# The first sixth of a fused attention and two-layer FFN kernel, issued from one list of 430 named operations

## The chip, the cores and the metric

The kernel runs on one core of one Trainium2 chip. The metric is the device time of one launch in microseconds (us), the median of several runs.

The engines are named as in the profile. PE is TensorE, which does the matmuls. PEld is its weight load, DVE is VectorE, ACT is ScalarE, POOL is GpSimd. SP issues most of the transfers. SPq and ACTq are the queues on which SP and ACT issue DMAs. Each engine works through its own instructions in program order, and semaphores make it wait for other engines or for transfers.

## The reference

`moe` and `moe2` are plain two-matrix layers over all tokens. There are 3072 tokens (4 batches of 768), model width 384 and inner width 2048. All numbers are float32.

```python
def _attn_ref(q, k, v, alpha):            # (4, 8, 768, 48) each
    state = np.zeros((B, H, D, D))
    for t in range(S):
        state = alpha[:, :, t, :, None] * state + np.einsum('bhd,bhe->bhde', k[:, :, t], v[:, :, t])
        y[:, :, t] = np.einsum('bhd,bhde->bhe', q[:, :, t], state)
    return y

def _moe_ref(x, w_in, w_out):
    h = x @ w_in
    g = np.maximum(0.01 * h, h)
    return g @ w_out

def _moe2_ref(x, w_in, w_out):
    h = x @ w_in
    g = np.where(h > 0.0, h, np.exp(np.minimum(h, 0.0)) - 1.0)
    return g @ w_out
```

The output is `_moe2_ref(_moe_ref(attention rows))`.

## The kernel before, in words

**Units and blocks.** A unit is 128 consecutive tokens of one batch, with all eight heads. There are 24 units, and four of them make a block of 512 tokens. The recurrence over a unit is done with matmuls. DVE builds running products of alpha with two scans, `E` and `F` (`prep_k`, `prep_F`), and scales k and q with them (`prep_k`, `prep_q`). PE forms the scores (`attn_sc`), DVE masks them (`attn_mask`), and PE forms the output (`attn_po`). The state goes from unit to unit: PE transposes k (`attn_pk`), ACT copies it out (`attn_kn`), PE multiplies it with v (`attn_pu`), and DVE adds it to the scaled old state (`attn_T` or `attn_carry`, then `attn_state`).

**Rows of x.** A unit's output is written as a high part (`attn_xh`, ACT) and the rest (`attn_rest` on PE and `attn_xl_act` on ACT in the first two blocks, `attn_xl` on DVE later). When the last unit of a block is done, `gather` moves some of the rows to other partitions with DMAs (`x<-x` in the profile). The block's FFN products read x only after that.

**FFN of layer 1.** The inner width is cut into 16 tiles m. `ffn1_h(j, m)` is a group of nine 128x512 matmuls for block j: for each of three 128-row parts of x, the products wh·xh, wl·xh and wh·xl (w is split into a high part wh and a low part wl, as x is). ACT copies the sum out (`ffn1_t`), DVE takes the maximum (`ffn1_max`), ACT rounds it to gh (`ffn1_gh`), DVE forms the rest gl (`ffn1_gl`). `ffn1_y(j, m)` is a second group of nine matmuls, from gh and gl into three sums `y` that collect over m.

**Conversion of the weights.** The weights come as 64-bit words. `stage1(m)` loads the words of tile m with five DMAs. Two ACT passes (`convert_p`), three DVE passes and an ACT cast to wh (`convert_a`), and a DVE subtraction for wl (`convert_b`) turn them into the two parts. In layer 1 all 16 tiles are converted in the first 151 us.

**Order.** Up to about 150 us the order is written out by hand: `quarter(u, i)` issues a quarter of unit u's attention and part of the preparation of unit u + 1, and `conv1.p`, `conv1.a`, `conv1.b` issue the conversions up to a number. Blocks 0 and 1 share this stretch. From `s = 4` to `s = 16` the main loop takes over with one y group, one h group and a conversion each. From `s = 17` on it issues an h group, an attention piece (`attn_pe` on PE, `attn_post` on ACT and DVE) and a y group per step. `in_order` then pins every engine to the order in which the code issued its instructions. Blocks 2 to 5 have their attention in the main loop, and layer 2 follows.

**Pools.** `pack` (alpha, k and q of a unit) and `v` have three buffers each. Two PSUM banks serve the h groups, three the y sums, three all of attention. Most of attention's intermediate tiles have one buffer.

Of the kernel before, what the change touches and what calls it, by code (L numbers as in the profile page):

```python
# [19 lines left out]
def attention_two_layers_kernel(  # L20
# [124 lines left out]
    def prep_k(u):  # L145
# [6 lines left out]
        pe = pe_p.tile([PR, NP, 1], F32, tag="pe", name="pe")  # L152
        nc.vector.tensor_scalar(pe, ext(E, 0)[:, :, 1:2], 1e24, 1e-24, ALU.min, ALU.max)
        nc.vector.reciprocal(ext(d1, 0)[:, :, 0:1], pe)
        e2 = E[:, 1:EXT].rearrange("p (g c) -> p g c", c=C + 1)
        nc.vector.tensor_mul(kS, kS, e2[:, :, 1:C + 1])
        st[u] = dict(kS=kS, qh=qh, pe=pe, alpha=al)
# [41 lines left out]

    def attn_mask(u):  # L200
        d = st[u]
        A = at_p.tile([128, 2, NP, C], F32, tag="A", name="A")
        for j, sc in enumerate(d.pop("sc")):
            nc.vector.tensor_mul(A[:, j], sc, causal.unsqueeze(1).to_broadcast([128, NP, C]))
        d["A"] = A

# [122 lines left out]
    def convert_p(raw, tp, ts, hi, lo):  # L329
        words = raw.rearrange("p (f t) -> p f t", t=2)  # L330
        rest = raw.bitcast(U16).rearrange("p (f t) -> p f t", t=4)[:, :, 1]
        nc.scalar.activation(tp.bitcast(F32), words[:, :, 1].bitcast(F32), ACTF.Copy, scale=2.0 ** -112)
        nc.scalar.activation(words[:, :, 0], rest, ACTF.Copy, scale=2.0 ** -13)

    def convert_a(raw, tp, ts, hi, lo):
        words = raw.rearrange("p (f t) -> p f t", t=2)
        nc.vector.tensor_scalar(ts, words[:, :, 1], -0x80000000, None, ALU.bitwise_and)
        nc.vector.scalar_tensor_tensor(  # L338
            out=tp, in0=tp, scalar=3, in1=ts, op0=ALU.logical_shift_left, op1=ALU.bitwise_or)
        nc.vector.tensor_tensor(out=ts, in0=tp, in1=words[:, :, 0], op=ALU.add)  # L340
        nc.scalar.copy(hi, ts.bitcast(F32))  # L341

    def convert_b(raw, tp, ts, hi, lo):
        nc.vector.tensor_sub(lo, ts.bitcast(F32), hi.bitcast(F32))

# [11 lines left out]
    def ffn1_h(j, m, ahead=0):  # L357
        xh, xl, n, _ = xt[j]
        hp = hbank(n, "hp")
        fill(hp, ahead)  # L360
        wh, wl = win[m]
        i = 0
        for kk in range(KD):
            for a, x in ((wh, xh), (wl, xh), (wh, xl)):
                nc.tensor.matmul(hp, lhsT=a[:, kk, :], rhs=x[:, kk, :n], start=(i == 0), stop=(i == 3 * KD - 1))  # L365
                i += 1
        steps[1, j, m] = hp

    def ffn1_t(j, m):
        t = g_p.tile([128, xt[j][2]], F32, tag="t", name="t")  # L370
        nc.scalar.copy(t, steps[1, j, m])  # L371
        steps[1, j, m] = t

    def ffn1_max(j, m):
        t = steps[1, j, m]
        nc.vector.scalar_tensor_tensor(out=t, in0=t, scalar=0.01, in1=t, op0=ALU.mult, op1=ALU.max)  # L376

    def ffn1_gh(j, m):
        gh = gs_p.tile([128, xt[j][2]], F32R, tag="gh", name="gh")
        nc.scalar.copy(gh, steps[1, j, m])  # L380
        steps[1, j, m] = steps[1, j, m], gh

    def ffn1_gl(j, m):
        t, gh = steps[1, j, m]
        gl = gs_p.tile([128, xt[j][2]], F32R, tag="gl", name="gl")
        nc.vector.tensor_sub(gl, t, gh.bitcast(F32))  # L386
        steps[1, j, m] = gh, gl
# [6 lines left out]

    FIRST = 4
# [5 lines left out]
    def ffn1_y(j, m):  # L401
        n = xt[j][2]
        gh, gl = steps.pop((1, j, m))
        first, last = parts(j, m)
        if first:
            ytiles[j] = [ps_y.tile([128, n], F32, tag=f"y{c}", name=f"y{c}") for c in range(KD)]
        wh, wl = wout[m]
        for c in range(KD):
            for i, (a, x) in enumerate(((wh, gh), (wl, gh), (wh, gl))):
                nc.tensor.matmul(  # L410
                    ytiles[j][c], lhsT=a[:, c * 128:(c + 1) * 128], rhs=x,
                    start=(first and i == 0), stop=(last and i == 2),
                )
        if last:
            t0 = blocks[j][0] * C
            dst = x2t[t0 // 512][:, :, t0 % 512:t0 % 512 + n]
            for c in range(KD):
                if j < 2 and m == KF - 1:
                    nc.vector.tensor_add(dst[:, c], ytiles[j][c], dst[:, c])
                elif c == 1 and j > 1:  # L420
                    nc.vector.tensor_copy(dst[:, c], ytiles[j][c])
                else:
                    nc.scalar.copy(dst[:, c], ytiles[j][c])  # L423
# [125 lines left out]
    def attn_post(u, i):  # L549
# [10 lines left out]
        else:  # L560
# [13 lines left out]
    def next_load(u):  # L574
        if u < NU:
            load_unit(u, eng=nc.scalar)
            load_v(u, eng=nc.scalar)
# [34 lines left out]
    def conv_args(layer, kind, m):  # L612
        i = kind == "out"
        w = (wout if i else win)[m]
        n = nconv[0] % (4 if layer == 1 else 3)
        nconv[0] += 1
        if layer == 1:
            tt = x2t[4 + n % 2].rearrange("p c f -> p (c f)").bitcast(I32)
            return staged[1, m], tt[:, 0:768], tt[:, 768:1536], both[m][0], both[m][1]
# [8 lines left out]

    class Conversions:
        def __init__(self, order):  # L630
            self.order = order
            self.done = [0, 0, 0]
            self.open = {}

        def p(self, upto):
            for i in range(self.done[0], min(upto, len(self.order))):
                self.open[i] = conv_args(1, *self.order[i])
                convert_p(*self.open[i])
                self.done[0] += 1

        def a(self, upto):
            self.p(upto)
            for i in range(self.done[1], min(upto, len(self.order))):
                convert_a(*self.open[i])
                self.done[1] += 1
                m = self.order[i][1]
                if m >= 2 and m + 2 < KF:
                    stage1(m + 2)

        def b(self, upto):  # L650
            for i in range(self.done[2], min(upto, self.done[1])):
                convert_b(*self.open.pop(i))
                kind, m = self.order[i]
                self.done[2] += 1


    class Flow:
# [8 lines left out]
        def start(self, k):  # L666
            raw, tp, ts, hi, lo = self.args[k] = conv_args(2, *self.order[k])
            words = raw.rearrange("p (f t) -> p f t", t=2)
            rest = raw.bitcast(U16).rearrange("p (f t) -> p f t", t=4)[:, :, 1]
            return [  # L670
                lambda: nc.scalar.activation(tp.bitcast(F32), words[:, :, 1].bitcast(F32), ACTF.Copy, scale=2.0 ** -112),
                lambda: nc.scalar.activation(words[:, :, 0], rest, ACTF.Copy, scale=2.0 ** -13)]
# [14 lines left out]
        def go(self, n):  # L687
            for i in range(n):
# [462 lines left out]
```

## Time and profile before

| | us |
|---|---|
| median of 3 runs | 937.37 (936.42 to 939.64) |
| profiled execution, its own time | 935.22 |
| its span, first to last instruction | 933.4 |
| PE busy | 898.0 (96%) |
| DVE busy | 542.7 (58%) |
| ACT busy | 449.9 (48%) |
| mean granted TensorE clock | 0.992 |

Busy shares are means over the whole span. The page of the profile also gives them in 40 slices of 23.3 us each. The first seven of them, about 160 us, hold the attention of the first eight units, the conversion of layer 1's weights, and the first FFN groups of blocks 0 and 1.

### The profile page before, as it was taken

The numbers are of one execution on the slowest core, as the hardware profiler recorded it, in microseconds if no ns is written. First come the engines' busy times: TensorE is split into PE (matmuls) and PEld (weight loads), VectorE is DVE, ScalarE is ACT, GpSimd is POOL, SyncE is SP. The second block draws the span as 40 slices with busy tenths as digits, with TensorE's granted clock in tenths as the row PEclk, the third lists the DMA queues.
The fourth block names the chain that finished last, engine by engine and source line by source line (L and its number), as shares of the span: only waits on it lengthen the run. The fifth ranks groups of instructions, "written<-read, shape, count | busy, mean of one in ns | idle before, by whom it ended". The sixth has DMA issues, their size and how long they took to land.

```text
span 933.4 us, 13414 instructions
## 1 busy us (share of the span) xinstructions
PE 898.0 (96%) x5283; PEld 732.0 (78%) x5283; DVE 542.7 (58%) x909; ACT 449.9 (48%) x816; POOL 1.4 (0%) x11
## 2 busy tenths in 40 slices
PE   7788999999999999999999999999999999999996
PEld 5666767787887878788888888888888888888896
DVE  7897787674665566376368888533433443443332
ACT  2545764222322322322357788746556566566442
POOL 0000000000000000000000000000000000000000
PEclk9999999999999999999999999999999999999999
DMA  9865431313123031321323242121110200200201
GB/s 239 211 181 148 128 111 28 84 44 77 43 77 86 1 86 43 77 78 35 98 72 104 84 119 62 31 46 31 30 34 21 54 11 21 54 21 1 34 1 38
DMA packets 55047, 63.97 MB, mean 69 GB/s; under 512 B 35456, under 2 KB 35968, under 8 KB 54976
## 3 DMA queue, kind: packets, MB, share of 16 engines
q1 hardware_dynamic: 51024, 49.61, 20.9%
q10 hardware_dynamic: 3952, 13.43, 5.3%
q8 instruction: 43, 0.70, 0.3%
q14 instruction: 28, 0.23, 0.1%
HBM read 54.37 MB, written 4.72 MB: 63 GB/s over the span
## 4 chain that ended last, share of the span: by engine, by line
PE 83%; DVE 8%; ACT 3%; DMA 3%; SPq 1%; issue 1%; ACTq 0%; DVEq 0%
PE hp L441 21%; PE y L410 18%; PE hp L365 16%; PE o L490 11%; PE oa L490 7%; PE oa L505 3%; PE po L256 2%; PE sc L228 2%; DVE x2t L338 1%; DMA x2t<-in_w_dram 1%; DVE x2t L340 1%; DMA x<-x 1%; PE o L505 1%; DVE E L151 1%; PE pu L275 1%
## 5 line engine op out<-in xcount | busy, mean ns | idle before, releaser
L365 PE MATMUL hp<-x,w 128*128 128x512 f32 x864 | 215.3, 393 | 7.5 <-DMA x<-x 4.7
L441 PE MATMUL hp<-x,w 128*128 128x512 f32 x864 | 212.3, 390 | 0.0
L365 PEld LDWEIGHTS hp<-x,w 128*128 128x128 f32 x864 | 162.2, 189 | 45.4 <-ACT w L341 4.8
L441 PEld LDWEIGHTS hp<-x,w 128*128 128x128 f32 x864 | 161.8, 188 | 33.4 <-DVE w L698 0.2
L410 PE MATMUL y<-gh,w 128*128 128x512 f32 x576 | 184.4, 401 | 3.6 <-ACT gh L380 2.9
L454 DVE SCALAR_TENSOR_TENSOR t<-t,hp 128x512 f32<-128x512 f32 x96 | 65.9, 687 | 144.0 <-ACT t L449 143.6
L380 ACT CAST gh<-t 128x512 fp32r<-128x512 f32 x96 | 59.7, 622 | 169.1 <-PE y L410 114.1
L386 DVE TENSOR_TENSOR gl<-t,gh 128x512 fp32r<-128x512 f32 x96 | 66.3, 691 | 111.8 <-ACT gh L380 111.2
L410 PEld LDWEIGHTS y<-gh,w 128*128 128x128 f32 x576 | 105.0, 189 | 29.3 <-ACT gh L380 4.9
L410 PE MATMUL y<-gl,w 128*128 128x512 f32 x288 | 113.3, 393 | 1.0 <-DVE gl L386 1.0
L465 DVE TENSOR_TENSOR gl<-t,gh 128x512 fp32r<-128x512 f32 x96 | 66.5, 692 | 66.0 <-ACT gh L459 66.0
L371 ACT COPY t<-hp 128x512 f32<-128x512 f32 x96 | 56.2, 586 | 100.0 <-PE hp L365 99.9
L448 ACT ACTIVATE t<-hp 128x512 f32<-128x512 f32 x96 | 57.3, 597 | 81.3 <-PE hp L441 81.3
L459 ACT CAST gh<-t 128x512 fp32r<-128x512 f32 x96 | 59.7, 622 | 69.7 <-PE o L490 22.8
L490 PE MATMUL o<-gh,w 128*128 128x512 f32 x288 | 88.8, 389 | 0.1
L376 DVE SCALAR_TENSOR_TENSOR t<-t 128x512 f32<-128x512 f32 x96 | 66.0, 687 | 37.8 <-ACT t L371 35.7
L410 PEld LDWEIGHTS y<-gl,w 128*128 128x128 f32 x288 | 54.3, 189 | 14.2 <-DVE gl L386 2.6
L490 PEld LDWEIGHTS o<-gh,w 128*128 128x128 f32 x288 | 54.0, 188 | 11.7 <-ACT x2t L423 0.5
L449 ACT ACTIVATE t<-t 128x512 f32<-128x512 f32 x96 | 60.7, 632 | 3.1
L490 PE MATMUL oa<-gh,w 128*128 128x512 f32 x192 | 59.1, 389 | 0.0
L490 PE MATMUL o<-gl,w 128*128 128x512 f32 x144 | 56.0, 389 | 0.0
L490 PEld LDWEIGHTS oa<-gh,w 128*128 128x128 f32 x192 | 36.0, 188 | 7.5
(130 smaller groups left out, 866.3 us busy)
## 6 DMA issues: line engine op xcount, KB each, us to landing
stg<-in_w_dram SPq DMA_DIRECT2D x28, 384.0 KB, 3.1
pack<-in_seqs_dram ACTq DMA_DIRECT2D x13, 674.2 KB, 5.0
x2t<-in_w_dram SPq DMA_DIRECT2D x20, 384.0 KB, 3.6
span<-in_seqs_dram SPq DMA_DIRECT2D x24, 226.2 KB, 2.6
pack<-in_seqs_dram SPq DMA_DIRECT2D x8, 674.2 KB, 7.3
x2t<-in_w_dram SPq DMA_DIRECT2D x32, 144.0 KB, 2.7
out_dram<-osb SPq DMA_DIRECT2D x60, 64.0 KB, 2.0
vt<-in_vals_dram ACTq DMA_DIRECT2D x13, 288.0 KB, 5.3
```

The costliest lines, as they stand in the source:

```text
L365: nc.tensor.matmul(hp, lhsT=a[:, kk, :], rhs=x[:, kk, :n], start=(i == 0), stop=(i == 3 * KD - 1))
L376: nc.vector.scalar_tensor_tensor(out=t, in0=t, scalar=0.01, in1=t, op0=ALU.mult, op1=ALU.max)
L380: nc.scalar.copy(gh, steps[1, j, m])
L386: nc.vector.tensor_sub(gl, t, gh.bitcast(F32))
L410: nc.tensor.matmul(ytiles[j][c], lhsT=a[:, c * 128:(c + 1) * 128], rhs=x, start=(first and i == 0), stop=(last and i == 2),)
L441: nc.tensor.matmul(hp, lhsT=a[:, kk, :], rhs=x[:, kk, :], start=(i == 0), stop=(i == 3 * KD - 1))
L448: nc.scalar.activation(t, hp, ACTF.Relu, scale=-1.0)
L449: nc.scalar.activation(t, t, ACTF.Exp, scale=-1.0)
L454: nc.vector.scalar_tensor_tensor(out=t, in0=t, scalar=-1.0, in1=hp, op0=ALU.add, op1=ALU.max)
L459: nc.scalar.copy(gh, t)
L465: nc.vector.tensor_sub(gl, t, gh.bitcast(F32))
L490: nc.tensor.matmul(otiles[j][c], lhsT=a[:, c * 128:(c + 1) * 128], rhs=x, start=(m == 0 and i == 0), stop=(m == KF - 1 and i == 2),)
```

## The change

The hand-written order up to `s = 16` is replaced by one string, `STARTUP`, of 430 names. Each name is a single operation on one engine (or a set of DMAs) with its unit, tile or block: `E.5` is the first scan of unit 5, `hA.0.3` the first part of h group (0, 3), `hi.7` the cast of tile 7's weights. A table `first` maps the names to functions, a loop calls them, and `in_order` pins the result. For this, `prep_k` is cut into `prep_E`, `prep_pe` and `prep_kS`, `attn_mask` into two halves, and the conversion into seven functions of one pass each.

An FFN group can now be issued in two parts. For h these are the six matmuls with wh and then the three with wl. For y they are the six with gh and then the three with gl. In the list all h and y groups are issued so. The matmuls themselves and their number stay.

In the main loop, the attention pieces are advanced by one at `s = 17` and `s = 18`, and a second piece of one step is issued behind the y group. In blocks 2 to 5, the last unit of a block now forms its low part and issues the gather ahead of the state update. Its loads for a later unit go behind the gather on SP's queue and not on ACT's queue.

```diff
+    def ffn1_h(j, m, ahead=0, halves=(0, 1)):
         xh, xl, n, _ = xt[j]
-        hp = hbank(n, "hp")
-        fill(hp, ahead)
+        if 0 in halves:
+            steps[1, j, m] = hp = hbank(n, "hp")
+            fill(hp, ahead)
+        hp = steps[1, j, m]
         wh, wl = win[m]
...
+        terms = [(kk, a, x) for kk in range(KD) for a, x in ((wh, xh), (wl, xh), (wh, xl))]
+        if len(halves) == 1:
+            terms = [t for t in terms if (t[1] is wl) == halves[0]]
+        for i, (kk, a, x) in enumerate(terms):
+            nc.tensor.matmul(hp, lhsT=a[:, kk, :], rhs=x[:, kk, :n], start=(0 in halves and i == 0),
+                             stop=(1 in halves and i == len(terms) - 1))
...
+    STARTUP = """
+        E.0 pe.0 F.0 kS.0 q.0 E.1 sc.0 pk.0 pe.1 kn.0 F.1 kS.1 mask0.0 q.1 pk.1 pu.0 mask1.0 E.2 sc.1 kn.1 more.0
...
+        S.3 q.4 xh.3 rest.3 E.5 xl.2 xl.3 j1.1 pk.4 gather.0 p1.2 more.2 kn.4 sc.4 lo.0 hA.0.0.7 hB.0.0 T.4 and.2
...
+        gl.0.10 gh.0.11 j2.14 yB.0.10 and.15 j1.15 hi.14 p2.15 lo.14 j2.15 hi.15 q.8 hA.0.14 hB.0.14 lo.15 piece.8.0
+        gh.0.12 t.0.13 t.0.14 gl.0.11 yA.0.11 gl.0.12 max.0.13 max.0.14 gh.0.13 gh.0.14 post.8.0 gl.0.13 gl.0.14
+        yB.0.11 yA.0.12 yB.0.12
+"""
...
             attn_xh(u, xh, off)
+            ends = u == blocks[j][0] + blocks[j][1] - 1
+            if ends:
+                attn_xl(u, xh, xl, off)
+                gather(t, blocks[j][1] * C, swapped=True)
             attn_state(u)
             if not last:
                 attn_carry(u + 1)
-            attn_xl(u, xh, xl, off)
+            if not ends:
+                attn_xl(u, xh, xl, off)
             st.pop(u)
-            if u == blocks[j][0] + blocks[j][1] - 1:
-                gather(t, blocks[j][1] * C, swapped=True)
-            next_load(u + 3)
+            next_load(u + 3, nc.sync if ends else nc.scalar)
...
+        for name in STARTUP.split():
+            f, *args = name.split(".")
+            first[f](*map(int, args))
         in_order()
...
-        pieces = [(u, i) for u in range(UB + blocks[1][1], NU) for i in range(3)]
+        pieces = [(u, i) for u in range(UB + blocks[1][1], NU) for i in range(3)][1:]
...
-                i, of = (s - KF + 1, KF - LA - 2) if s < 2 * KF else (m + 1, KF - LA - 2)
+                i, of = (s - KF + 1 + (s in (KF + 1, KF + 2)), KF - LA - 2) if s < 2 * KF else (m + 1, KF - LA - 2)
```

**Place 1, PE, from the first FFN group on.** Before: `hp` are the h groups, `w_0_104` and `w_0_105` the high and the low part of tile 0's weights, `w_1_...` those of tile 1, `po` is unit 4's attention output, and the x7 row is filler ahead of the first group.

```order
L354 MATMUL hp<-minus 112x448 x7
L365 MATMUL hp<-x,w_0_104 128x512
L365 MATMUL hp<-x,w_0_105 128x512
L365 MATMUL hp<-x,w_0_104 128x512 x2
L365 MATMUL hp<-x,w_0_105 128x512
L365 MATMUL hp<-x,w_0_104 128x512 x2
L365 MATMUL hp<-x,w_0_105 128x512
L365 MATMUL hp<-x,w_0_104 128x512
L365 MATMUL hp<-x,w_1_106 128x512
```

The same place of the change:

```order
L380 MATMUL hp<-minus 112x448 x7
L394 MATMUL hp<-x,w_0_104 128x512 x6
L394 MATMUL hp<-x,w_0_105 128x512 x3
L265 MATMUL po<-A,vt 64x128
```

The three matmuls with the low part now come last in the group, and unit 4's output stands between the h groups of tiles 0 and 1, where before the two groups followed each other.

**Place 2, SP, around block 0's gather.** Before: `x<-x` is the gather (three of its six DMAs), `x2t_138` and `x2t_139` are the words of weight tiles 2 and 3, `pack` and `vt` are a unit's data. The first `pack` row is unit 6.

```order
L125 DMA pack<-in_seqs_dram 112x1541
L139 DMA vt<-in_vals_dram 128x576
L590 DMA x2t_138<-in_w_dram 48x768
L591 DMA x2t_138<-in_w_dram 16x768
L590 DMA x2t_138<-in_w_dram 48x768
L591 DMA x2t_138<-in_w_dram 16x768
L592 DMA x2t_138<-in_w_dram 128x768
L324 DMA x<-x 16x2x512 x3
L139 DMA vt<-in_vals_dram 128x576
L590 DMA x2t_139<-in_w_dram 48x768
```

And of the change, where unit 6 is the `pack` row behind the gather:

```order
L660 DMA x2t_138<-in_w_dram 128x768
L658 DMA x2t_139<-in_w_dram 48x768
L659 DMA x2t_139<-in_w_dram 16x768
L658 DMA x2t_139<-in_w_dram 48x768
L659 DMA x2t_139<-in_w_dram 16x768
L660 DMA x2t_139<-in_w_dram 128x768
L333 DMA x<-x 16x2x512 x3
L125 DMA pack<-in_seqs_dram 112x1541
L139 DMA vt<-in_vals_dram 128x576
```

Weight tile 3 moved ahead of the gather, and unit 6's load moved from ahead of tile 2 to behind the gather.

**Place 3, DVE, at the end of the conversions.** Before: `w_15_135` is the low part of the last tile, `t<-t` a maximum, `gl` the rest of g, `A` the mask of unit 8, `E` the first scan of unit 9.

```order
L340 ISA x2t_141<-x2t_139,x2t_141 128x1536
L376 SCALAR_TENSOR_TENSOR t<-t 128x512
L344 TENSOR_TENSOR w_15_135<-x2t_141,w_15_134 128x768
L386 TENSOR_TENSOR gl<-t,gh 128x512
L204 TENSOR_TENSOR A<-sc_1394,causal 128x512
L204 TENSOR_TENSOR A<-sc_1395,causal 128x512
L151 SCALAR_TENSOR_TENSOR E<-pack,d_97 112x517
```

And of the change:

```order
L360 ISA x2t_141<-x2t_139,x2t_141 128x1536
L179 TENSOR_TENSOR pack<-pack,F 112x512
L366 TENSOR_TENSOR w_15_135<-x2t_141,w_15_134 128x768
L412 TENSOR_TENSOR gl<-t,gh 128x512 x2
L404 SCALAR_TENSOR_TENSOR t<-t 128x512 x2
L210 TENSOR_TENSOR A<-sc_1356,causal 128x512
L210 TENSOR_TENSOR A<-sc_1357,causal 128x512
L151 SCALAR_TENSOR_TENSOR E<-pack,d_97 112x517
L157 TENSOR_SCALAR pe<-E 112x4
L158 RECIPROCAL d_98<-pe 112x4
L163 TENSOR_TENSOR pack<-pack,E 112x512
L412 TENSOR_TENSOR gl<-t,gh 128x512 x2
```

Two FFN tiles are now in flight behind the last conversion. The two `gl` rows at the end, of tiles 13 and 14, stand behind the mask and the scan, where before only one tile's `gl` followed the conversion and it came ahead of them.

## Rows read from the trace of the kernel before

**Rows 1.** The page's first two parts: busy times, then tenths in 40 slices.
```profile
PE 898.0 (96%) x5283; PEld 732.0 (78%) x5283; DVE 542.7 (58%) x909; ACT 449.9 (48%) x816; POOL 1.4 (0%) x11
...
PE   7788999999999999999999999999999999999996
...
DVE  7897787674665566376368888533433443443332
```
**Rows 2.** Busy time by stretch (us from the start, length, engines, clock, DMA).
```profile
0.00:4.73 4.73, 1.81 (x5) 1.54 (x6) 1.06 (x6) 1.58 (x2) 1.19 (x9) 1.00 0.57 163
4.73:39.84 35.11, 26.89 (x314) 20.87 (x313) 31.64 (x52) 12.06 (x20) 0.00 (x0) 0.95 1.01 250
39.84:78.92 39.08, 33.61 (x281) 25.30 (x281) 34.82 (x57) 18.69 (x30) 0.00 (x0) 1.00 0.53 149
78.92:149.61 70.69, 63.83 (x301) 48.56 (x301) 57.21 (x77) 44.34 (x67) 0.00 (x0) 0.98 0.45 127
149.61:154.48 4.87, 4.38 (x14) 3.17 (x14) 4.80 (x8) 0.71 (x2) 0.00 (x0) 0.65 0.00 0
154.48:200.00 45.52, 43.86 (x395) 35.20 (x393) 29.21 (x53) 13.12 (x29) 0.11 (x1) 1.00 0.22 61
200.00:527.23 327.23, 325.31 (x2186) 263.54 (x2187) 200.76 (x362) 118.81 (x241) 0.11 (x1) 1.00 0.26 68
```
**Rows 3.** PE's waits, 0 to 150 us (total us, times, longest).
```profile
PE pu L275 <- DVE A L204: 4.4, 4, 1.8
PE y L410 <- ACT gh L380: 2.9, 1, 2.9
...
PE hp L365 <- DMA x<-x: 2.8, 2, 2.2
```
**Rows 4.** DVE groups of 0 to 154.48 us: mean ns, idle before and its releaser.
```profile
L344 DVE TENSOR_TENSOR w<-x2t,w 128x768 fp32r<-128x768 f32 x16 | 15.2, 956 | 4.1 <-ACT w L341 4.0
L386 DVE TENSOR_TENSOR gl<-t,gh 128x512 fp32r<-128x512 f32 x19 | 13.0, 686 | 3.8 <-ACT gh L380 3.2 <-PE y L410 0.7
L376 DVE SCALAR_TENSOR_TENSOR t<-t 128x512 f32<-128x512 f32 x19 | 13.0, 686 | 6.7 <-ACT t L371 6.7
L204 DVE TENSOR_TENSOR A<-sc,causal 128x512 f32<-128x512 f32 x18 | 11.5, 682 | 2.1 <-PE sc L182 2.1
L151 DVE TENSOR_TENSOR_SCAN E<-pack,d 112x517 f32<-112x517 f32 x9 | 11.1, 1228 | 2.6 <-DMA pack<-in_seqs_dram 2.6
```
**Rows 5.** Timeline of PE and SP around the first gather and the first h group.
```profile
35.40 2.33 SPq L324 DMA_DIRECT2D x<-x  x3
...
39.84 4.37 PE L365 MATMUL hp<-x,w 128*128 128x512 f32 x18 [2.15 <-DMA x<-x]
```
**Rows 6.** The chain that ended last, one h group behind a y group.
```profile
202.27 2.04 PE hp L365 x9
```
**Rows 7.** DMA issues of 0 to 160 us: median us to landing.
```profile
pack<-in_seqs_dram SPq DMA_DIRECT2D x8, 674.2 KB, 7.3
```
**Rows 8.** Busy time by stretch around PE's two low-clock stretches.
```profile
86.50:89.20 2.70, 2.69 (x6) 2.11 (x7) 2.02 (x4) 1.49 (x3) 0.00 (x0) 0.50 0.86 227
...
147.00:150.60 3.60, 2.34 (x52) 1.48 (x50) 3.17 (x5) 1.94 (x3) 0.00 (x0) 1.00 0.00 0
150.60:154.00 3.40, 3.40 (x9) 2.51 (x9) 3.33 (x7) 0.00 (x0) 0.00 (x0) 0.53 0.00 0
```
**Rows 9.** PE's waits, 149 to 200 us.
```profile
PE pk L190 <- DVE A L204: 1.7, 1, 1.7
PE hp L365 <- ACT w L341: 0.8, 1, 0.8
```
**Rows 10.** PE's waits from 200 us on.
```profile
PE hp L365 <- DMA x<-x: 1.9, 3, 0.9
```
**Rows 11.** Timeline of DVE ahead of a gather of the main loop.
```profile
293.50 0.35 DVE L311 TENSOR_TENSOR S<-pu,carried 112x192 f32<-112x192 f32 x1
293.89 0.36 DVE L218 TENSOR_TENSOR carried<-S,pe 112x192 f32<-112x192 f32 x1
```

More of the change, by code (lines that the diff above doesn't have):

```diff
@@ L198, in attn_kn, with mask_half @@
             d["kn"] = kn
-    def attn_mask(u):
[L201 to L205, printed above, removed]
+    def mask_half(u, j):
+        d = st[u]
+        if "A" not in d:
+            d["A"] = at_p.tile([128, 2, NP, C], F32, tag="A", name="A")
+        nc.vector.tensor_mul(d["A"][:, j], d["sc"][j], causal.unsqueeze(1).to_broadcast([128, NP, C]))
+    def attn_mask(u):
+        mask_half(u, 0)
+        mask_half(u, 1)
     def attn_T(u):
@@ L399, in parts, with ffn1_y @@
         return m == 0 or (j < 2 and m == FIRST), m == KF - 1 or (j < 2 and m == FIRST - 1)
-    def ffn1_y(j, m):
+    def ffn1_y(j, m, copy=True, halves=(0, 1)):
         n = xt[j][2]
-        gh, gl = steps.pop((1, j, m))
+        gh, gl = steps["gh", j, m], steps.get(("gl", j, m))
         first, last = parts(j, m)
-        if first:
+        if first and 0 in halves:
             ytiles[j] = [ps_y.tile([128, n], F32, tag=f"y{c}", name=f"y{c}") for c in range(KD)]
         wh, wl = wout[m]
[L408 to L416, printed above, removed]
-            for c in range(KD):
[L418 to L423, printed above, removed]
@@ new lines, in ffn1_y @@
+        terms = [(c, a, x) for c in range(KD) for a, x in ((wh, gh), (wl, gh), (wh, gl))]
+        if len(halves) == 1:
+            terms = [t for t in terms if (t[2] is not gh) == halves[0]]
+            terms.sort(key=lambda t: t[1] is wl)
+        begun = set()
+        for i, (c, a, x) in enumerate(terms):
+            nc.tensor.matmul(
+                ytiles[j][c], lhsT=a[:, c * 128:(c + 1) * 128], rhs=x,
+                start=(first and 0 in halves and c not in begun),
+                stop=(last and 1 in halves and c not in [t[0] for t in terms[i + 1:]]),
+            )
+            begun.add(c)
@@ new lines, in ffn1_y, with y_copy @@
+        if 1 in halves:
+            del steps["gh", j, m], steps["gl", j, m]
+        if last and copy:
+            for c in range(KD):
+                y_copy(j, m, c)
+    def y_copy(j, m, c):
+        n = xt[j][2]
+        t0 = blocks[j][0] * C
+        dst = x2t[t0 // 512][:, c, t0 % 512:t0 % 512 + n]
+        if j < 2 and m == KF - 1:
+            nc.vector.tensor_add(dst, ytiles[j][c], dst)
+        elif c == 1 and j > 1:
+            nc.vector.tensor_copy(dst, ytiles[j][c])
+        else:
+            nc.scalar.copy(dst, ytiles[j][c])
@@ L627, in conv_args @@
         return raw, tp, ts, flat(w[0]), flat(w[1])
[L629 to L654, printed above, removed]
     class Flow:
@@ L1046, in attention_two_layers_kernel @@
                 post_h(n)
[L1047 removed]
+                for p in now[:1]:
                     attn_pe(*p)
                 if m < KF - 1:
[L1050 removed]
+                    for p in now[:1]:
                         attn_post(*p)
@@ L1053, in attention_two_layers_kernel @@
                 if m == KF - 1:
-                    for p in now:
+                    for p in now[:1]:
                         attn_post(*p)
+                for p in now[1:]:
+                    attn_pe(*p)
+                    attn_post(*p)
             if ph == 2 and m >= KF - 10 and m % 2 == 0:
```

296 lines of the change are left out of this document (98 added, 198 removed).

## The prediction

> **What bounds the kernel now.** I began with the page. PE is busy for 96% of the span, and its slices stand at 9 from the seventh on, except for the last [rows 1]. So only the beginning has time to give. There, PE's slices stand at 7 and 8 and those of DVE mostly between 6 and 8, so neither engine is full, and both are needed.
>
> The busy time by stretch says how much is lost and on whom [rows 2]. I cut at 39.84 us, where the first h group of the FFN starts [rows 5], at 78.92, where block 1's first h group starts, at 149.61, where the h group (0, 15) starts, which is the first group behind the list, and at 154.48, where DVE has done all that the list contains. PE is idle for 39.08 − 33.61 = 5.47 us in the third stretch and 70.69 − 63.83 = 6.86 us in the fourth. DVE, from its first scan at 4.73 to 154.48, is busy for 31.64 + 34.82 + 57.21 + 4.80 = 128.47 us of 149.75 and idle for 21.28.
>
> The waits name the reason. PE waits for masks (4.4 us), for gh (2.9) and for the gathers (2.8) [rows 3], which are things that DVE and ACT make. DVE waits in its turn, for a maximum's input 6.7 us, for ACT's cast of the weights 4.0, for gh 3.2, for scores 2.1 [rows 4], while it has other work further down its own queue: conversions of later tiles, scans of later units. The engines run in order, so that work stays behind the waiting instruction. The loss is one of order, and from 200 us on there is little of it: 327.23 − 325.31 = 1.92 us up to 527.23 [rows 2].
>
> **The change, part by part.** It adds and removes no computation up to the list's end. DVE, ACT and PE run the same passes, and the two parts of an FFN group together are the same nine matmuls. What can change is idle time, so each term is an idle time of before and the part of it that I expect back. All terms are against the profiled execution, 935.22 us. It lies 2.15 below the median of 937.37, so the forecast is that median less the sum.
>
> *Up to the first h group: 0.* The gather of block 0 needs four units of attention in a chain, and was issued at 35.40 [rows 5]. In this stretch DVE is idle for only 35.11 − 31.64 = 3.47 us [rows 2], and the list puts more of units 4 and 5 and of tile 1 ahead of the gather than the old order did. The bounds are 3.47 earlier and, for one more load ahead of the gather on SP (place 2), some 3 later. I take 0, as gains and added work cancel.
>
> *Between the first h group and (0, 15): 10.0.* Two floors limit how early (0, 15) can start. For PE, all its busy time of the third and fourth stretch stays: 33.61 + 63.83 = 97.44, so 39.84 + 97.44 = 137.28 us, which is 12.33 earlier than 149.61. For DVE, the list ends no sooner than 4.73 + 128.47 = 133.20. Behind the last operation that PE needs (`gl.0.12`) the list has two maxima, two masks, a scan and two `gl`, 2 × 0.686 + 2 × 0.682 + 1.228 + 2 × 0.686 = 5.3 us [rows 4], and some smaller ones, so `gl.0.12` could be done at about 128. A y group is nine matmuls of an h group's size, 2.04 us [rows 6], of which a part is left then, so DVE would allow about 130. PE's floor is thus the later one, and DVE may still idle for 7 us before it holds PE up. That is a third of its present 21.28, so not all of PE's waits will go. The forms point the right way: in the list a maximum, its `gh` and its `gl` stand several other DVE operations apart, where before DVE often ran into them directly, and a group split into high and low parts lets PE start when the cast is done and the subtraction is not (place 1). One known wait is new: unit 6's load now goes behind the gather (place 2). Issued at about 38, with 7.3 us to landing [rows 7], it is there at about 45, and DVE, which comes to unit 6's scan at about that time, has the rest of tile 2 and the first maximum behind it. I count 2.3 us of waits as left, for this one and the many cross-engine hand-overs, so 12.33 − 2.3 = 10.0. The bounds are 4 (two thirds of the waits come back in other places) and 13.7 (all of it, and also the 1.35 us lost to the low clock at 86.5 to 89.2, half of 2.70 [rows 8]).
>
> *From (0, 15) to 200 us: 2.6.* Before, (0, 15) waited 0.8 for the last cast [rows 9] and ran at a granted clock of 0.53 for 3.40 us [rows 8], which cost about 1.6. At 172 PE waited 1.7 for a mask [rows 9] that stood behind other DVE work. Now the last conversion is done before (0, 15), and `s = 19` has no attention piece. Counting only idle and the clock, 0.49 + 1.6 + 1.66 = 3.75 could go [rows 2, 8]. Against it stands place 3: `gl.0.13` and `gl.0.14` are behind the mask and scan, and the y group (0, 13) may wait about 1 us for them. 3.75 − 1.15 = 2.6, bounds 0 and 3.75.
>
> *Gathers of the main loop: 1.5.* PE waited for three of them, 1.9 us in all, the longest 0.9 [rows 10]. Where the block's last unit isn't the last of a batch, the gather now goes ahead of the state update and the carry, 0.35 + 0.36 = 0.71 us [rows 11], and no load runs beside it. The moved loads serve a unit several steps later, and SP has nothing else to issue for the FFN then, so I cost the move at nothing. I take 1.5 of 1.92, with bounds of 0.5 and 1.92.
>
> The sum is 10.0 + 2.6 + 1.5 = 14.1: 935.22 − 14.1 = 921.1 for an execution like the profiled one, and 937.37 − 14.1 = 923.3 against the median. I predict 923.
>
> **A rule against it.** PE's clock falls even where waits are short. From 147.0 to 150.6 PE was busy for 2.34 of 3.60 us, with waits of at most 0.8, and then ran at 0.53 [rows 8, 9]. From 39.84 to 78.92 it waited 5.47 us and kept 1.00 [rows 2]. The Trainium skill, page "TensorE: Matmul & The Clock Gate", section "A second HAM failure mode: psum-queue depth-cycling", says that a PE which is idle for moments between groups of matmuls, often enough, swings between its two levels and loses throughput though no single wait is long. By that rule a list that splits every group and puts a possible wait between the parts could lose what it gains. The trace agrees at 147 and disagrees over the stretch at 39.84.
>
> **The rivals.**
> *The waits only move* (PE finds other operations late, since DVE has merely 7 us to spare). For it: both engines would have to be nearly full from 40 to 135, with 17 in-order hand-overs of y groups and conversions between them. Then half to a third of the 12.33 comes back, and about half of the other two terms: 4.5 + 2 = 6.5, so 931.
> *Nothing in the end.* If the first h group slips by 5 us behind the longer SP queue and the waits move as above, gains and losses cancel: 935 to 940.
> *Slower: the low clock.* Its place is the FFN groups between 40 and 137 us. They are 19 h and 17 y groups at 2.04 us, 73.4 us of work [rows 6], and each us of granted half clock costs half a us. Before, 2.70 + 3.40 = 6.1 us were slow after 39.84 [rows 8]. It takes 28 us more to use up the 14.1, so it decides from about a third of these groups on. With half of them slow, 36.7 us of work takes twice as long, so the kernel loses 36.7 − 14.1 = 22.6 and ends at 960. With 40 us of granted half clock it loses 20 − 14.1 = 6 and ends at 943. Against it: most of PE's waiting so far left the clock at 1.00.
> *More comes back.* If all three terms reach their upper bounds, 13.7 + 3.75 + 1.92 = 19.4, so 918.
>
> **How the numbers follow.** Any difference of under 0.3%, 2.8 us, can't be told from no change here. I give the forecast 0.50 (920 to 927), more coming back 0.10, the waits that only move 0.27 (927 to 934), no difference 0.06, the low clock 0.07. The first three are faster, together 0.87. The range has to leave out 2 in 10: from 916, two us below the case at 918, to 933, within the case of waits that move. The likeliest case's own range is 920 to 927.
>
> **What would show it.** In the profile after, the first h group starts at 37 to 43, block 1's first h group at 72 to 76 where it was 78.92, and (0, 15) at about 139.6. DVE's idle time up to the end of the list falls from 21.28 to about 10. The waits for a maximum's input, for the cast of the weights and for gh shrink by more than half. The 1.7 us wait at 172 is gone, and PE's wait for the gathers after 200 us falls under 0.5. From 200 us to the end the length is the same within 2 us. Wrong would be a first h group later than 45, which puts the fault with SP's queue and the loads; a granted clock of under 0.9 over the stretch up to 137, which is the clock; or DVE idle for 15 us and more, which says that the order trades one wait for another.

## The result and the profile after

The changed kernel takes 924.56 us, median of 6 runs (921.18 to 927.0). The kernel before, run beside it, takes 937.33 (935.91 to 940.21). The ratio is 0.9849, 95% interval 0.9831 to 0.9868: 12.8 us less, 1.3 less than the 14.1 of the sum. In a second series (e0 below) it was 15.2 us less. The profiled execution took 924.84 us with a span of 923.1.

First the page of the changed kernel, its busy times, slices and clock (tenths, 23 us to a slice).

```profile
PE 900.7 (98%) x5283; PEld 738.9 (80%) x5283; DVE 539.3 (58%) x909; ACT 448.9 (49%) x816; POOL 1.4 (0%) x11
...
PE   7899999999999999999999999999999999999996
...
DVE  6889996665664566565378887533443443443332
...
PEclk7789999999999999999999999999999999999999
```

PE's slices reach 9 from the third on, where they were there from the fifth before [rows 1]. But DVE's first slice is lower than before, and the clock's first three are 7, 7 and 8. What follows is the busy time by stretch, cut at the first h group (46.58), at block 1's first h group (82.25) and at (0, 15) (143.81).

```profile
4.73:46.58 41.85, 34.36 (x298) 26.88 (x297) 34.33 (x57) 12.65 (x20) 0.00 (x0) 0.75 0.91 206
46.58:82.25 35.67, 33.44 (x288) 25.54 (x288) 31.50 (x51) 18.48 (x30) 0.00 (x0) 0.91 0.59 165
82.25:143.81 61.56, 61.42 (x310) 50.05 (x310) 58.30 (x85) 43.53 (x67) 0.00 (x0) 1.00 0.54 147
143.81:200.00 56.19, 55.51 (x454) 44.57 (x454) 35.34 (x64) 15.96 (x34) 0.11 (x1) 1.00 0.19 54
200.00:515.00 315.00, 315.00 (x2139) 255.94 (x2136) 194.68 (x352) 116.01 (x238) 0.11 (x1) 1.00 0.26 70
```

Against [rows 2], the first stretch is longer (41.85 against 35.11) and the two behind it are shorter (97.23 together against 109.77). From 82.25 on PE has next to no idle time. The gain is thus made behind the first h group, and a part of it is lost ahead of it. These are PE's waits from 0 to 150 us, then DVE's from 4.73 to 143.81 (total us, times, longest).

```profile
PE hp L394 <- DMA x<-x: 3.5, 2, 2.4
...
PE pk L196 <- DVE A L210: 2.3, 1, 2.3
PE po L265 <- DVE A L210: 1.4, 2, 0.9
PE po L308 <- ACT x L301: 1.0, 2, 0.7
PE pu L284 <- DVE A L210: 0.8, 1, 0.8
```
```profile
DVE A L210 <- PE po L265: 5.3, 3, 3.3
DVE E L151 <- DMA pack<-in_seqs_dram: 2.7, 2, 2.3
DVE A L210 <- PE sc L188: 2.5, 2, 2.3
DVE S L320 <- PE pu L284: 1.6, 1, 1.6
DVE t L404 <- ACT t L399: 1.2, 3, 0.6
DVE gl L412 <- PE y L467: 1.1, 1, 1.1
DVE w L366 <- ACT w L363: 1.0, 2, 0.7
```

PE's waits for gh and for weights [rows 3, 9] are gone. DVE's waits for a maximum's input fell from 6.7 to 1.2, those for the cast of the weights [rows 4] to 1.0, and those for gh are gone. At the head of DVE's list stands a new wait: masks that wait for `po`, 5.3 us. The next timeline shows where it arises: PE of the changed kernel, and then the first of unit 1's two masks on DVE.

```profile
12.63 1.01 PE L196 MATMUL pk<-ident,pack 112*128 112x112 f32 x4 [2.32 <-DVE A L210]
13.57 1.09 PE L284 MATMUL pu<-vt,kn 128*64 128x48 f32 x16
14.59 2.84 PE L188 MATMUL sc<-pack 48*128 48x128 f32 x16
17.36 1.97 PE L265 MATMUL po<-A,vt 128*64 128x128 f32 x16
...
46.58 1.80 PE L394 MATMUL hp<-x,w 128*128 128x512 f32 x3 [2.41 <-DMA x<-x]
```
```profile
19.38 0.69 DVE L210 TENSOR_TENSOR A<-sc,causal 128x512 f32<-128x512 f32 x1 [3.32 <-PE po L265]
```

A has one buffer, and it is held until `po.0` has read it. In the list `sc.1` stands ahead of `po.0`. At this low clock `sc.1` takes 2.84 us and `po.0` 1.97, where the same sixteen matmuls take 1.16 and 1.09 us in e3 (below), whose granted clock is 1.00 from 12.5 to 20 us. So DVE stands still for 3.32 us. The first h group comes 6.74 us later than before; what of that is due to this place is the question of the experiments.

### The profile page after: what moved, and what is told of

It is laid out like the page before. It is cut to its first block, busy times and chain, and to the rows that moved or that the text cites. A ratio compares the mean times of both kernels' runs of the same rounds, so it can differ in the third digit from the quotient of the medians.

```text
span 923.1 us, 13446 instructions
## 1 busy us (share of the span) xinstructions
PE 900.7 (98%) x5283; PEld 738.9 (80%) x5283; DVE 539.3 (58%) x909; ACT 448.9 (49%) x816; POOL 1.4 (0%) x11
## 4 chain that ended last, share of the span: by engine, by line
PE 91%; DVE 3%; DMA 2%; issue 1%; ACT 1%; SPq 0%; DVEq 0%; ACTq 0%
PE hp L506 21%; PE y L467 20%; PE hp L394 20%; PE o L555 11%; PE oa L555 7%; PE po L265 3%; PE oa L570 3%; PE sc L237 2%; DMA x<-x 1%; PE pu L284 1%; PE sc L188 1%; PE o L570 1%; PE pk L196 1%; DMA x2t<-in_w_dram 1%; PE po L245 1%
## 5 line engine op out<-in xcount | busy, mean ns | idle before, releaser
L467 PE MATMUL y<-gh,w 128*128 128x512 f32 x576 | 177.2, 398 | 0.7 <-DVE x2t L484 0.7
L467 PE MATMUL y<-gl,w 128*128 128x512 f32 x288 | 107.3, 392 | 0.0
```

The costliest lines, as they stand in the source:

```text
L467: nc.tensor.matmul(ytiles[j][c], lhsT=a[:, c * 128:(c + 1) * 128], rhs=x, start=(first and 0 in halves and c not in begun), stop=(last and ...
```

## The experiments

Three theories of the late first group. **1:** the low clock behind PE's 2.3 us wait. **2:** the order, with `po.0` behind `sc.1` and more work ahead. **3:** SP's queue. The table has the times (each ratio is to the kernel before beside it, which had medians of 938.08, 936.34 and 937.63 in the three series) and what the profiled execution shows: the start of the first h group, of (0, 15), the time between, and the time from (0, 15) to the end of the span. All are us.

| kernel | median | ratio (95%) | first h | (0, 15) | between | to the end |
|---|---|---|---|---|---|---|
| before | 937.33 | | 39.84 | 149.61 | 109.77 | 783.79 |
| changed | 924.56 | 0.9849 (0.9831 to 0.9868) | 46.58 | 143.81 | 97.23 | 779.29 |
| e0 changed, again | 921.11 | 0.9840 (0.9814 to 0.9867) | 43.53 | 139.79 | 96.26 | 779.01 |
| e1 filler behind `pk.0` | 920.78 | 0.9807 (0.9785 to 0.9829) | 43.07 | 139.94 | 96.87 | 779.06 |
| e3 head in the hand's order | 922.50 | 0.9828 (0.9806 to 0.9851) | 38.94 | 142.23 | 103.29 | 778.47 |
| e4 before + gather edit | 937.69 | 1.0000 (0.9987 to 1.0012) | 41.03 | 154.14 | 113.11 | 781.66 |
| e5 gather edit undone | 922.60 | 0.9860 (0.9828 to 0.9891) | 46.27 | 143.67 | 97.40 | 779.83 |
| e6 h and y whole | 929.24 | 0.9897 (0.9879 to 0.9915) | 44.05 | 148.80 | 104.75 | 779.10 |
| e7 `po.0` ahead of `sc.1` | 920.12 | 0.9830 (0.9801 to 0.9859) | 40.49 | 138.44 | 97.95 | 778.96 |
| e8 pieces at old steps | 922.04 | 0.9851 (0.9823 to 0.9879) | 43.28 | 140.32 | 97.04 | 779.78 |
| e10 e7 + gather filler | 918.60 | 0.9805 (0.9772 to 0.9838) | 41.15 | 138.25 | 97.10 | 778.85 |
| e11 changed + gather filler | 921.22 | 0.9830 (0.9797 to 0.9863) | 43.82 | 139.59 | 95.77 | 779.21 |
| e13 y whole | 923.39 | 0.9844 (0.9813 to 0.9874) | 46.01 | 145.03 | 99.02 | 779.37 |
| e14 h whole | 924.71 | 0.9862 (0.9830 to 0.9894) | 44.46 | 143.63 | 99.17 | 779.17 |

**Filler behind `pk.0`.**
```diff
-        E.0 pe.0 F.0 kS.0 q.0 E.1 sc.0 pk.0 pe.1 kn.0
+        E.0 pe.0 F.0 kS.0 q.0 E.1 sc.0 pk.0 fill.11 pe.1 kn.0
...
+            "fill": lambda n: fill(hw, n),
```


> Eleven filler matmuls stand behind pk.0, where TensorE of the changed kernel waits 2.32 us for mask0.0 and behind which its granted clock is 0.53 from 12.6 to 26.3 us. Theory 1 (the low clock makes the first FFN group late): the clock stays over 0.9 up to 40 us, sc.1 falls from 2.84 to about 1.2 us, VectorE's 3.3 us wait for po.0 to about 1, the first FFN group starts at 40 to 42 us instead of 46.6, and the time is 919 to 921. Theory 2 (the order itself: more VectorE work ahead of the first FFN group and one buffer for A behind po.0): the clock may rise, the first group stays at 45 to 47 us and the time at 924 to 925. Theory 3 (SyncE's queue): as theory 2, with the wait of the gather's first load unchanged.

The wait is covered, but the clock falls all the same: 0.76 from 12.5 to 20 us and 0.80 from 20 to 28. The first group starts at 43.07, 0.5 us earlier than in the second profile of the changed kernel. So the 2.3 us wait alone is not what brings the clock down, and covering it does not bring the first group back. Whether the low clock makes the group late this run can't say, since the clock fell. The ratio is 0.004 below that of the changed kernel, but against the second measurement of it the intervals overlap. I don't count it as shown.

**The head in the hand's order.** The 95 names ahead of `hA.0.0.7` are in the order that `quarter` had; here the beginning:
```diff
-        E.0 pe.0 F.0 kS.0 q.0 E.1 sc.0 pk.0 pe.1 kn.0 F.1 kS.1 mask0.0 q.1 pk.1 pu.0 mask1.0 E.2 sc.1 kn.1 more.0
-        po.0 pu.1 S.0 xh.0 kS.2 rest.0 pe.2 mask1.1 T.1 mask0.1 po.1 xl.0 E.3 xh.1 F.2 rest.1 kS.3 q.2 pk.2 p1.0
+        E.0 pe.0 kS.0 F.0 q.0 sc.0 pk.0 kn.0
+        pu.0 E.1 pe.1 kS.1 mask0.0 mask1.0 pk.1 kn.1 po.0 F.1 S.0 q.1 sc.1 xh.0 rest.0 more.0 stage.1 xl.0
...
```


> The changed kernel, with the 95 names ahead of the first FFN group in the order that they had by hand; all behind them stays as in the list. Theories 1 and 2: the first FFN group starts at 40 to 41 us instead of 46.6; if the 12.5 us that came back behind it are the work of the rest of the list, they come back all the same, and the time is 918 to 920. Rival: a part of the 12.5 us is work that the list does ahead of the first group, so that what is won ahead is lost behind: 923 to 925. Theory 3: the order of loads is as by hand too, so that it does not tell it from theories 1 and 2.

The two ends of it, from PE's timeline (the second is (0, 15)):
```profile
38.94 3.75 PE L394 MATMUL hp<-x,w 128*128 128x512 f32 x9 [3.75 <-DMA x<-x]
...
142.23 2.21 PE L394 MATMUL hp<-x,w 128*128 128x512 f32 x9
```
The first group is back at 38.94, yet (0, 15) comes only 1.58 us earlier than in the first profile of the changed kernel and 2.44 later than in the second. The stretch between takes 103.29 us instead of 96 to 97. The rival holds by the profile: some 6 of the 12.5 to 13.5 us that came back behind the first group had been paid for ahead of it. DVE's work shows the larger part: in that stretch it is busy for 93.46 us here, and for 89.80 and 89.38 in the two profiles of the changed kernel, so about 4 us of its work had moved ahead. The time, 922.50, lies between the ranges of the two theories.

**The gather edit alone**, on the kernel before. The lines of the diff for the gather, without the rest.


> The kernel before, with the main loop's gather put ahead of the loads and nothing else. If the gather waits are a term of their own: 1.9 us less than before (935.4), and no TensorE wait for the gathered x after 200 us. Rival: another wait ends there in their place: 937, no change.

The wait for the gathered x after 200 us is gone, and from (0, 15) to the end takes 2.13 us less. The median is the same: 937.69 against 938.08. Every engine's order is that of the kernel before up to the first gather of the main loop, so its beginning shows what one order does in another execution:
```profile
41.03 5.37 PE L365 MATMUL hp<-x,w 128*128 128x512 f32 x12 [4.52 <-DMA x<-x]
...
83.42 4.62 PE L365 MATMUL hp<-x,w 128*128 128x512 f32 x18 [0.71 <-DMA x<-x]
...
154.14 0.50 PE L365 MATMUL hp<-x,w 128*128 128x512 f32 x1 [0.77 <-ACT w L341]
```
(0, 15) is 4.53 us later than before, where it stood at 149.61 [rows 2], as PE waits longer for the gather (4.52 us against 2.15 [rows 5]) and runs at a lower clock behind it (0.67 from 36 to 46 us, against 1.00). A single profile of the beginning can thus be off by some 4 us. Why the medians don't show the 2.13 us stays open: the interval excludes it, and the noise of the beginning should average out.

**The changed kernel again**, not edited.


> The changed kernel, not edited, as the base for the runs beside it and as a second profile. What differs between its two profiles is what one program does from run to run. If the late first FFN group (46.6 us) belongs to the program, it stands at 44 to 47 us again, with VectorE's wait for po.0 at 2 to 3.5 us and (0,15) at 143 to 149; if it was an accident of one execution, at 39 to 42. Time: 922 to 927.

The same stretches in this execution:
```profile
4.73:43.53 38.80, 29.40 (x299) 23.01 (x297) 34.09 (x58) 12.83 (x21) 0.00 (x0) 0.87 0.87 222
43.53:79.00 35.47, 33.13 (x291) 25.24 (x291) 32.36 (x52) 19.41 (x31) 0.00 (x0) 0.95 0.62 170
79.00:139.79 60.79, 60.65 (x307) 49.40 (x306) 57.02 (x84) 42.83 (x66) 0.00 (x0) 1.00 0.54 147
```
The first group and (0, 15) both came earlier than the ranges for a late group. So the late group belongs to the program, but not all 6.7 us of it. Seven profiles have this list up to there (the changed kernel, e0, e5, e6, e8, e13, e14). Their first group starts at 43.3 to 44.5 in four and at 46.0 to 46.6 in three. What tells these apart is the clock from 28 to 36 us, here of the changed kernel's first profile, and then of e0:
```profile
12.50:20.00 7.50, 6.69 (x52) 5.43 (x52) 4.15 (x10) 1.12 (x2) 0.00 (x0) 0.50 1.05 220
...
28.00:36.00 8.00, 7.69 (x79) 6.58 (x78) 5.91 (x11) 1.34 (x2) 0.00 (x0) 0.57 1.02 215
```
```profile
12.50:20.00 7.50, 6.61 (x59) 5.48 (x61) 4.55 (x11) 1.12 (x2) 0.00 (x0) 0.54 1.04 267
...
28.00:36.00 8.00, 6.11 (x98) 5.00 (x96) 7.97 (x16) 3.89 (x6) 0.00 (x0) 1.00 0.66 140
```
All seven are slow from 12.5 to 20 (0.50 to 0.62). The three late ones are slow a second time, at 0.57 or 0.58, and their first group is some 2.5 us later in the mean. Theory 3 is answered here too, by the first profile of the changed kernel:
```profile
40.09 1.26 ACT L312 CAST x<-po 112x512 fp32r<-112x512 f32 x2
...
40.96 0.37 SPq L660 DMA_DIRECT2D x2t<-in_w_dram  x1
41.39 2.00 ACTq L333 DMA_DIRECT2D x<-x  x3
41.42 2.25 SPq L333 DMA_DIRECT2D x<-x  x3
```
SP has five loads of weights ahead of the gather, the last issued at 40.96 for 0.37 us, and the gather goes out at 41.39 on ACT and 41.42 on SP. But ACT's last cast of x, which the gather needs, ends only at 40.09 + 1.26 = 41.35. SP's queue was not late. From the gather's issue to the first group it took 5.16 us, against 4.44 before [rows 5], so at most 0.7 of the 6.7 us arose behind the issue.

**`po.0` ahead of `sc.1`.**
```diff
-        ... pu.0 mask1.0 E.2 sc.1 kn.1 more.0
-        po.0 pu.1 S.0 xh.0 ...
+        ... pu.0 mask1.0 po.0 E.2 sc.1 kn.1 more.0
+        pu.1 S.0 xh.0 ...
```


> The changed kernel, with po.0 ahead of sc.1 (and of E.2) in the list, no filler matmul. Theory 2 (the one buffer of A is held until po.0, which stands behind sc.1 on TensorE): VectorE's wait of 3.3 us for po.0 falls under 1, the first FFN group starts 2 to 4 us earlier than in the unedited run beside it, and the time is 2 to 4 us lower. Theory 1 (the granted clock alone, after TensorE's 2.3 us wait at 10 us, which stays): the clock is still about 0.5 from 13 to 27 us, the first group is less than 1 us earlier, and the time is the same within 1 us.

```profile
8.60 2.08 PE L188 MATMUL sc<-pack 48*128 48x128 f32 x16
...
14.44 1.90 PE L265 MATMUL po<-A,vt 128*64 128x128 f32 x15
16.27 1.16 PE L188 MATMUL sc<-pack 48*128 48x128 f32 x16
...
40.49 3.69 PE L394 MATMUL hp<-x,w 128*128 128x512 f32 x9 [1.89 <-DMA x<-x]
```
DVE's wait for `po.0` is gone (in its place it waits 1.4 us for `sc.1`), and the first group starts 3.0 us earlier than in e0, as theory 2 said. But the slow stretch also came at another time: `sc.0` took 2.08 us here, and from 16 us on all is fast. So this run doesn't part the order from the clock. The run e10, which has the same order, does so only in part. Its clock was 0.77 from 12.5 to 20, where DVE waited 1.6 for `sc.1` and not for `po.0`, and its first group starts at 41.15. But from 20 to 28 its clock was 1.00, where that of e11, the same with the old order, was 0.74. That a slow stretch costs less with `po.0` first is likely and not shown. At the end 1.35 of the 3.0 us are left in (0, 15), and the time is 1 us lower than e0's, less than the interval and less than the 2 to 4 us expected.

**The pieces at their old steps.**
```diff
-                i, of = (s - KF + 1 + (s in (KF + 1, KF + 2)), KF - LA - 2) if s < 2 * KF else (m + 1, KF - LA - 2)
+                i, of = (s - KF + 1, KF - LA - 2) if s < 2 * KF else (m + 1, KF - LA - 2)
```


> The changed kernel, with the attention pieces of the main loop's first steps at their old steps. Term B of the prediction (2.6 us between (0,15) and 200 us): if the advance of the pieces is what brings it, TensorE waits 1 to 2 us for A near 170 us again and the time is 1.5 to 3 us above the unedited run beside it. Rival: the list's head start alone brings it, and the time is the same within 1 us.

PE's waits from 150 to 600 us, first of e8, then of the changed kernel run again:
```profile
PE pk L196 <- DVE A L210: 1.7, 1, 1.7
```
```profile
PE y L467 <- DVE x2t L484: 0.7, 1, 0.7
PE o L555 <- ACT x2t L488: 0.4, 1, 0.4
```
The 1.7 us wait is back, but two others, 1.1 us together, go. From (0, 15) to the end takes 779.78 instead of 779.01. The edit is worth 0.8 by the profile and 0.9 us by the medians, which is inside the interval.

**The gather edit undone**, in the changed kernel.


> The changed kernel, with the main loop's gather and load as before. By the waits of the profile, TensorE waits 1.5 to 2 us again for the gathered x after 200 us, and the time is 1.5 to 2 us above that of the unedited run beside it. Rival, by the run of the gather edit alone (937.69 against 938.08): less than 1 us, since it disappears between runs of the same program.

PE's waits from 150 to 600 us, the one for the gathered x:
```profile
PE hp L394 <- DMA x<-x: 1.0, 2, 0.5
```
PE waits twice instead of the three times of [rows 10], 1.0 us in all where I had expected 1.5 to 2, and from (0, 15) to the end is 0.8 longer than in e0. By the medians it is 1.5 us, inside the interval.

**Whole groups.** Each `hA`/`hB` and `yA`/`yB` pair becomes one whole group at the second part's place.
```diff
-        ... hA.0.1 j2.2 t.0.0 lo.1 ... max.0.0 hB.0.1 hA.0.2 rest.4 hB.0.2 ...
+        ... j2.2 t.0.0 lo.1 ... max.0.0 h.0.1 rest.4 h.0.2 ...
```


> The changed list, with each FFN product issued whole at the place of its second part. If the parts carry the gain: TensorE waits for weights and for VectorE's maximum again, and from the first FFN group to (0,15) take 103 to 109 us instead of 97.2: 930 to 936. Rival, the order of the other names carries it: 97 to 99 us there, 924 to 927.

> The changed kernel with each y product issued whole at the place of its second part, the h products in parts. With both whole the time was 4.5 to 5 us above that of the changed kernel. If the y parts carry that (a first part that needs gh only starts without gl): 4 to 5 us above, from the first FFN group to (0,15) 103 to 105 us. If the h parts carry it: less than 1 us above, 97 us there.

> The changed kernel with each h product issued whole at the place of its second part, the y products in parts. If the h parts carry the 4.5 to 5 us (a first part that needs the high half of the weights only starts without the low half): 4 to 5 us above the changed kernel; if the y parts do: less than 1 us above.

With both whole, the stretch between takes 104.75 us, and the ratio is 0.005 higher: 4.5 us of the gain are lost. The waits of e6 from 46 to 150 us show on whom:
```profile
PE sc L188 <- DVE pack L179: 2.9, 2, 1.7
PE y L442 <- DVE gl L412: 1.9, 1, 1.9
```
Neither is a wait for weights or for a maximum, which I had expected. And the waits are only a half of it. PE is idle for 6.14 us in that stretch, against 2.37 and 2.48 in the two profiles of the changed kernel. It is busy for 98.61 us against 94.86 and 93.78, at a mean clock of 0.93 against 0.97 and 0.98.

With one kind whole, the stretch takes 99.0 (y) or 99.2 (h), 2 to 3 us more than in the changed kernel instead of 8, and the ratios can't be told from its own. I had expected one of them to carry it, and that falls. That PE has something to issue as long as either kind is in parts is how I read it; these are single profiles, and no run shows it. Nor did a run issue whole groups at the place of the first part.

What e6 keeps is a ratio of 0.9897, 9.7 us less than before. It has the gather edit and the advanced pieces too, worth 0.8 to 2.1 and 0.8 us by the profiles. So some 7 to 8 us belong to the order of the names, by difference.

**Filler ahead of the two gathered groups.**
```diff
-        S.3 q.4 ... sc.4 lo.0 hA.0.0.7 hB.0.0 T.4 and.2
+        S.3 q.4 ... sc.4 lo.0 hA.0.0.16 hB.0.0 T.4 and.2
...
-        yB.0.2 hA.1.0.4 hB.1.0 ...
+        yB.0.2 hA.1.0.9 hB.1.0 ...
```


> The run with po.0 ahead of sc.1, and more filler matmuls ahead of the two groups that wait for a gathered x: 16 instead of 7 at (0,0), 9 instead of 4 at (1,0). In the run with po.0 first alone TensorE idles there 1.9 and 1.2 us, and the nine matmuls of (0,0) take 3.7 us instead of 2.2. If the idle costs its clock: the waits are gone, the nine take 2.2 us, (0,15) starts 1.5 to 2 us earlier (at 136.5 to 137), and the time is 918 to 919. Rival: VectorE is the limit there (it idles 0.03 of 10 us between 36 and 46), so that (0,15) stays at 138 to 139 and the time at 920.

> The changed kernel with the same added filler matmuls (16 at (0,0), 9 at (1,0)), the order not touched. As for the run above: (0,0)'s nine matmuls take 2.2 us instead of 3.3 to 4.2 after the wait, and the time is 1 to 2 us lower than that of the changed kernel; by the rival, that VectorE is the limit there, no change within 1 us.

The first group in e10, whose nine matmuls take 3.11 us with a last short wait, where e7's took 3.69:
```profile
41.15 0.70 PE L394 MATMUL hp<-x,w 128*128 128x512 f32 x2 [0.97 <-DMA x<-x]
42.01 2.25 PE L394 MATMUL hp<-x,w 128*128 128x512 f32 x7 [0.16 <-DMA x<-x]
```
The clock from 36 to 46 us rose from 0.83 to 1.00, but (0, 15) moved from 138.44 to 138.25 in one pair and from 139.79 to 139.59 in the other. The rival had said that (0, 15) would stay, with DVE as the limit. The first half of that holds. In e11 PE is 1.17 us ahead of e0 at 72 us and 0.30 ahead at block 1's first h group, which in both waits for its own gather (1.0 and 1.2 us). So the lead is lost just ahead of that gather. That DVE takes it is not shown. e10 has the lowest median of all, 918.60, and beats the kernel before by 1.6 to 2.3%. Over the changed kernel its lead of 3 to 4 us is not shown, since the intervals overlap.

## Why the prediction was right, and where a step failed

*Up to the first h group: 0.* This step failed, in "I take 0, as gains and added work cancel". The slip is 6.74 us in the profile and 3.4 to 6.7 over seven profiles. Its bound of 3 came from SP's queue, and "later than 45" was to put the fault there. The runs put it elsewhere. The list sets `sc.1` ahead of `po.0` while A has one buffer, and PE is slow in just that place. With `po.0` first and another course of the clock 3.0 us of it came back (e7), and where the second slow stretch comes the group is some 2.5 us later. How much is the order and how much the clock stays open. What the step did not see is that DVE would wait for `po` (5.3 us), and that TensorE's clock in the first stretch, 0.95 before, would be 0.75 and in the second profile 0.87.

*First h group to (0, 15): 10.0.* It was 12.54 in the first profile and 13.51 in the second. The first two terms are not independent, as e3 shows: some 6 us of this had been paid for ahead of the first group. PE's floor was none either. "All its busy time" of the two stretches was to stay, 97.44 us, but it was 94.86 and 93.78, with more matmuls in it (598 and 598, against 582 [rows 2]). A part of that is how busy time comes out where a group waits. Two rows of the kernel before show an h group with a wait inside:
```profile
139.16 0.50 PE L365 MATMUL hp<-x,w 128*128 128x512 f32 x1 [0.46 <-ACT w L341]
140.15 2.11 PE L365 MATMUL hp<-x,w 128*128 128x512 f32 x8 [0.49 <-DVE w L344]
```
That is 2.61 us busy, where nine matmuls without a wait show 2.21 (e3's row at 142.23). The sum of the first two terms is what counts, and it was right: (0, 15) stands at 141.90 in the mean of four profiles of the unedited list up to there (changed, e0, e5, e8) and at 151.88 in the mean of two of the old order (before, e4), which is 9.98 earlier, against 10.0. That it agrees so closely is luck: an error of 3.4 to 6.7 us in the first term and one of 2.5 to 3.5 us in the second went against each other, and two profiles of the old order alone differ by 4.53 us. Where (0, 15) was forecast at about 139.6, it came at 143.81 and 139.79. By idle time the sum is right in size. PE's idle from 4.73 to (0, 15) was 144.88 − 124.33 = 20.55 us [rows 2], and in the two profiles it is 139.08 − 129.22 = 9.86 and 135.06 − 123.18 = 11.88. In the first of them PE's busy time is 4.9 us longer, at a mean clock of 0.90 there against 0.98 before.

*(0, 15) to the end: 2.6 + 1.5 = 4.1.* 783.79 became 779.29 and 779.01, so 4.5 to 4.8. The gather edit brought 2.13 of it on its own (e4) and 0.8 beside the rest (e5), the pieces 0.8 (e8). The remainder would be the list's lead, as the last conversion no longer stands in front of (0, 15); no run shows it alone.

*The signs.* DVE's idle time from 4.73 to (0, 15), near the list's end, was 14.95 us, and 11.59 in the second profile, where I had said about 10, with 15 as the mark of a fault. The first profile is at that mark, and its waits for `po` are 5.3 of it. Block 1's first h group started at 82.25 and not at 72 to 76: the slip of the first stretch carried over. The first group later than 45 came too, but the fault was not with SP's queue. The waits for a maximum, the cast and gh shrank by more than half, the wait at 172 is gone, and the gathers' waits after 200 us are 0.

*The rivals.* "The waits only move" happened in one place (masks for `po`, 5.3 us) and not in the FFN. "Nothing in the end" had its slip of 5 us and more in the first profile, but behind it the gain came. The rival of the low clock was placed in the FFN groups, and there it came only from 46 to 54 us (0.58, behind the wait for the gathered x): from 82.25 on the clock is 1.00 with PE busy for 61.42 of 61.56 us. From the first h group to 137 us it was 0.97 and 0.98 in the two profiles, so that rival's sign, under 0.9, did not come. Its price had a slip: the 28 us of half clock that use up 14.1 us hold 14 us of full-speed work, a fifth of the 73.4 and not a third. The low clock came in the attention ahead of them, where I had not looked, for a few us. The Trainium skill, page "TensorE: Matmul & The Clock Gate", section "A second HAM failure mode: psum-queue depth-cycling", reports such swings for a kernel whose PE was often idle for short moments between groups of matmuls. By that rule the split groups would have swung had PE waited between the parts. Behind 82.25 it was idle for 0.14 us, so this trace doesn't test the rule there.

*A reading.* The prediction has PE's slices at 9 from the seventh on. In [rows 1] they are there from the fifth, so fewer slices had time to give; the terms were taken from [rows 2] and don't change.

## What to carry to other kernels

The start of the first big product is no milestone when an order is compared: e3 brought it 4.6 us forward from e0's place and came 2.4 us later to (0, 15). Compare at an operation behind which the two orders are the same, and against two or three profiles. Splitting a product by what its operands wait for lets PE start on a part of them: with both kinds whole 4.5 us of the gain went, with one kind whole none that the times can tell. Where a buffer is single, look at who waits for its reader: behind the next unit's work it made DVE wait for 3.3 and 2.9 us in the two profiles. Whether moving it gains time was not shown here.

## What the runs showed of the hardware

The granted clock of the first 40 us can't be read off from PE's busy time there. These are the windows from 12.5 to 20 us of e1, then of e3:
```profile
12.50:20.00 7.50, 5.74 (x69) 4.67 (x69) 5.36 (x11) 1.12 (x2) 0.00 (x0) 0.76 1.06 256
```
```profile
12.50:20.00 7.50, 5.72 (x86) 4.58 (x85) 7.43 (x14) 2.23 (x4) 0.00 (x0) 1.00 1.06 265
```
PE was busy for 5.74 and 5.72 of 7.50 us, with waits of at most 0.9 in e1 and up to 1.33 in e3. Yet e1's clock fell and e3's did not (the same busy time held 69 matmuls at the lower clock, and 86 at the other). In all seven profiles of the list it lay at 0.50 to 0.62 there. What decides it is open.

Nor does the clock's row tell all in the first 16 us. This is e7, where `sc.0` took 2.08 us against 1.16 in the changed kernel, and the row gives 1.00 all the same:
```profile
8.50:16.00 7.50, 6.41 (x56) 5.54 (x56) 7.36 (x14) 1.06 (x2) 0.00 (x0) 1.00 1.04 250
```
There the durations of like matmuls say more than the clock. And one order, run twice, had (0, 15) at 149.61 and 154.14, which is more than the gather edit or the pieces are worth.
